# Four orders of work dealt anew in a block-recurrent attention and SwiGLU kernel: middle batches, last batch and states

## The chip, the cores and the metric

The kernel runs on one core of one Trainium2 chip. The time is the device time of one execution in microseconds (us). TensorE (PE, with its weight loads PEld), VectorE (DVE), ScalarE (ACT), GpSimd (POOL) and SyncE (SP, which here only issues DMAs) run side by side, each through its own instructions in order, and wait for one another through semaphores.

## The reference, cut to what matters

```python
# x (8, 8, 512, 64) and state (8, 8, 32, 64); scale = 1 / 8
a  = softmax(scale * x @ state^T)     # over the 32 state rows
xread = a @ state                     # 512 rows a batch and head
a2 = softmax(scale * state @ x^T)     # over the 512 tokens
sread = a2 @ x                        # 32 rows a batch and head
y  = concat([xread, sread], axis=2)   # 544 rows a batch -> (4352, 512)
n  = y / sqrt(mean(y * y) + 1e-6) * rms_g
g, v = n @ w_gate, n @ w_val          # (512, 1536) each
out = (g * sigmoid(g) * v) @ w_out    # (1536, 512)
```

All of it is float32.

## The kernel before, in words

The work goes batch by batch (b = 0 to 7; the 512 token rows of each), and the 256 state rows of all batches come at the end. Batch 0 is computed while the weights are converted, with an order of its own (`ORDER`). From batch 1 on, a batch has two stages, and the attention of the next batch is woven into them.

Hidden stage (`hidden_seven`, L704). The 12 column blocks of the hidden layer are taken in six pairs, mp = 0 to 5. Gate and value products of a pair are built by a scheme with seven half-size products instead of eight, so each pair needs seven products of 128x256 on TensorE (L714, stream h), sums of its weight blocks (vs, L594 to L597 on GpSimd), sums of the token blocks (`slot_sums`, L632 to L635 on GpSimd), three adds on the way out (L776 on VectorE), three copies out of PSUM (L760, L763, L765 on ScalarE, stream t), a Silu (L767) and two multiplications into hb (L789). Pairs 3 to 5 also form sums for the next stage (L795, L801). The banks in PSUM are few: two for x, one for y, one for z, so a product waits until the copy or add of an earlier one has read its bank. Token weights of a batch are its own: `own_weights` (L555) multiplies state rows into the weights (L567, TensorE), ScalarE copies the result to v (L579).

Projection stage (`project_twice`, L985). hb times w_out by the same scheme applied twice: seven outer products o, each of seven inner ones of 3 x 2 matmuls of 128x128 (L1016, stream p). Each outer product needs four quarter sums (L1064, L1066, L1068, L1070 on VectorE, stream k, in two buffers), some need half sums (L1075). Results p1, u2, p5 and c21 are copied to `kept` tiles (L1026, ScalarE), added to (L1056, VectorE), combined by four adds on GpSimd (L1042, L1044, L1046, L1047) and stored (L1124, SP queue). The `kept` tiles of p1, u2 and c21 share two buffers with g of the hidden stage, so a copy into g waits for a store.

Attention of batch b+1 (`tokens_read` L403, stream a; `states_read` L457, stream s): x goes through VectorE transposes (L328) and a round trip through DRAM (L330, L335: four transfers into xG on the ScalarE queue) to the scores (L345), softmax steps on VectorE (L354 to L433), the read (L440), squares (L447), their sum (L450 to L389), the root on GpSimd (L289), its spread over rows (L296) and the scaling (L453); the states' read is L509, with a transpose at L524.

Queues: SP issues, in its own order, the weights w_m of a pair (`fetch`, L187, 1 MB each, three buffers), the quarter sums of w_out (`fetch_quarters`, L962, three buffers), the stores, the state rows (L127) and x (L132).

The order of all this is written out by hand: each step of each stream is one letter in a string, and the loop takes the next step of the stream that the letter names. A letter thus fixes an instruction's place on its own engine against the other streams; it holds no engine back for another. `FIRST` is the order of batch 1, `PERIOD` of batches 2 to 6, `LAST` of batch 7, `STATES` of the state rows. `LAST` has no next batch: its stream a is the norm of the states (L532 to L547, L699) and the first sums of w for the states (L671 to L677). In `STATES`, y is the other sums of w and p, c, k are those of `project_seven` (L862: products L879, adds L924 and L931, copies L916).

| letter | stream | engine |
|---|---|---|
| h, t, u | products, copies with Silu, sums of the hidden stage | PE, ACT, DVE |
| v, x | own weights: products; copies and sums | PE; ACT and POOL |
| w | slot sums and first own weights of the next batch | POOL, PE |
| p, c, k, o | projection: products, copies, sums, stores | PE, ACT, DVE, SP |
| a, s | attention of the next batch | all |
| f, g, l | fetches of weights, of quarter sums; loads of x and states | SP |
| y | sums of w for the states | DVE |

Of the kernel before, what the change touches and what calls it, by code (L numbers as in the profile page):

```python
# [28 lines left out]
)  # L29

PERIOD = (
    "vfhththahhtalhhuxxutthufxtvhhhtahahuuuuuthauhattahhhhxthhuxuutxhuhuttuvkkxxxvxha"
    "hhthhauuuxxhkaatuhkuuthuaattaaahuahuhuthtsusushhhuutthhughuuptpaauufhuagpkuppkkp"
    "saakfgkkappcpkpakkckpkppapppppckkkkpakppppppkppkpppcaaaaaksssaaaaakpppckkpppksap"
    "pkskkagggcksakaakppppaooaoposkppppgkkkpasakoawsswxosspxfxlccoowxxxf"
)

FIRST = (
# [4 lines left out]
    "xosspxfxlccoowxxxf"  # L43
)
LAST = (
    "vfhththhhthhuxxutthufxtvhhhthhuuuuuthuhtthhhhxthhuxuutxhuhuttuvkkxxxvxhhhthhuuux"
    "xhktuhkuuthuattahuhuhuthtuuhhhuutthhughuuptpuufhuagpkuppkkpkfgkkppcpkpakkckpkppp"
    "ppppckkkkpkppppppkppkpppcakaakpppckkpppkppkkkgggckkakppppooopokppppgkkkpakoopcco"
    "o"
)  # L50
STATES = (
    "hyyyyhthyytthhhuuhtuhththhytuuhuuhthuhhtthyuhyyutyhhhuuuttyuhhutyyhhthuhyhuhuttu"
    "yhuhttyuhuhuuhuthhyuthythytuhuuhuhutuuphuupcpkpcpukkcpkpkpc"
)


# [1191 lines left out]
```

## Time and profile before

| what | us |
|---|---|
| median of three runs | 770.23 |
| the three runs | 770.18, 770.23, 770.73 |
| the profiled execution, its own time | 770.64 |
| its span, first to last instruction | 768.9 |
| PE busy in the span | 752.1 |
| DVE busy | 608.3 |
| ACT busy | 350.5 |
| POOL busy | 292.0 |
| first L714 product of batches 3, 4, 5, 6 | 305.8, 387.5, 469.2, 551.4 |
| granted TensorE clock, share of full speed | 1.000 |

Busy time is the time in which an engine has an instruction at work; a matmul that is held inside TensorE's pipeline counts as busy. The timeline gives, for each group of equal instructions, start and length in us, and in brackets the idle time before it with the instruction whose end released it. A group of matmuls ends later than the next one starts, since they are pipelined: the distance from start to start is the time that TensorE spends on a group. One matmul of the program in float32 shows as two records.

### The profile page before, as it was taken

Reading aid. Unit: us, or ns where it says so; the run is one execution under the profiler, and the core shown is the slowest. Engines: PE = TensorE matmul, PEld = TensorE weight load, DVE = VectorE, ACT = ScalarE, POOL = GpSimd, SP = SyncE. Lnnn points to the kernel's source line nnn. Section 1 sums busy time; section 2 is a strip of 40 time slices with the busy share of each in tenths; the row PEclk is TensorE's granted clock in tenths of the full one; section 3 lists DMA queues with packets and bytes.
Section 4 is the critical chain, followed back from the end, with each engine's and each line's share of the span. In section 5 each row is a group of like instructions: output and inputs, shape, how many; then the busy total and the mean of one; then the engine's idle time right before and its main releaser. Section 6 shows DMA issues by size and latency. Waiting matters only on the chain.

```text
span 768.9 us, 14347 instructions
## 1 busy us (share of the span) xinstructions
PE 752.1 (98%) x5608; PEld 595.0 (77%) x5608; DVE 608.3 (79%) x1000; ACT 350.5 (46%) x548; POOL 292.0 (38%) x379
## 2 busy tenths in 40 slices
PE   8899999999999999999999999999999999999998
PEld 7534434778877898879977997889878988899996
DVE  4999997589956996689957994799569975799562
ACT  5898974544245513653165424542355136511220
POOL 2000002984584226632474039402842266325400
PEclk9999999999999999999999999999999999999999
DMA  9787845745786167825683467616862665052311
GB/s 291 213 284 258 312 180 194 276 154 209 268 252 238 41 233 244 292 55 202 202 304 116 127 216 253 228 52 231 250 238 51 233 206 217 1 202 73 124 55 27
DMA packets 61890, 146.15 MB, mean 190 GB/s; under 512 B 15744, under 2 KB 32640, under 8 KB 54912
## 3 DMA queue, kind: packets, MB, share of 16 engines
q1 hardware_dynamic: 48704, 125.78, 47.8%
q10 hardware_dynamic: 13120, 19.47, 8.8%
q8 instruction: 44, 0.72, 0.4%
q14 instruction: 22, 0.18, 0.1%
HBM read 116.46 MB, written 28.77 MB: 189 GB/s over the span
## 4 chain that ended last, share of the span: by engine, by line
PE 62%; DVE 27%; POOL 4%; issue 3%; ACT 2%; DMA 1%; SPq 0%; DVEq 0%; ACTq 0%; POOLq 0%
PE f L714 26%; PE f L1016 14%; PE f L816 6%; PE pv L610 5%; DVE hb L789 3%; DVE hb L1075 3%; PE at L567 3%; PE f L879 2%; DVE h L1070 2%; PE pv L567 2%; DVE g L776 2%; DVE h L1064 2%; DVE hs L795 2%; DVE h L1066 2%; DVE kept L1056 1%
## 5 line engine op out<-in xcount | busy, mean ns | idle before, releaser
L714 PE MATMUL f<-aT_s,v 128*128 128x256 f32 x504 | 117.5, 380 | 0.0
L714 PEld LDWEIGHTS f<-aT_s,v 128*128 128x128 f32 x504 | 95.2, 190 | 18.5 <-ACT v L579 5.0
L776 DVE TENSOR_TENSOR g<-g,f 128x512 f32<-128x512 f32 (+1 forms) x96 | 61.9, 650 | 53.4 <-PE f L714 42.1
L1042 POOL TENSOR_TENSOR kept<-kept 128x256 f32<-128x256 f32 x28 | 23.5, 839 | 199.7 <-DVE z L428 113.1
L714 PE MATMUL f<-aT_t,vs 128*128 128x256 f32 x336 | 87.7, 385 | 0.9 <-ACT g L760 0.5
L767 ACT ACTIVATE hb<-g 128x1024 f32<-128x1024 f32 (+1 forms) x48 | 48.3, 1006 | 70.8 <-DVE g L776 70.7
L1016 PE MATMUL f<-w,h 128*128 128x128 f32 x588 | 75.3, 278 | 3.6 <-DVE h L1066 3.5
L714 PEld LDWEIGHTS f<-aT_t,vs 128*128 128x128 f32 x336 | 61.9, 190 | 19.3 <-issue 7.8
L1016 PEld LDWEIGHTS f<-w,h 128*128 128x128 f32 x588 | 69.8, 192 | 5.7 <-DVE h L1066 4.8
L1026 ACT COPY kept<-f 128x512 f32<-128x512 f32 (+1 forms) x56 | 28.9, 540 | 71.5 <-PE f L1016 56.2
L594 POOL TENSOR_TENSOR vs<-v 128x256 f32<-128x256 f32 x42 | 32.6, 776 | 68.0 <-ACT v L579 68.0
L579 ACT COPY v<-pv 128x512 f32<-128x512 f32 x42 | 22.7, 592 | 76.2 <-PE pv L567 76.2
L289 POOL TENSOR_TENSOR ri<-ss,mhalf 128x4 f32<-128x4 f32 x8 | 10.4, 1295 | 116.3 <-DVE ss L371 113.8
L714 PE MATMUL f<-aT_t,v 128*128 128x256 f32 x168 | 44.5, 387 | 1.5 <-DVE c L776 1.5
L816 PE MATMUL f<-wo,hb 128*128 128x512 f32 x96 | 44.4, 600 | 0.0
L765 ACT COPY g<-f 128x512 f32<-128x512 f32 (+1 forms) x48 | 26.9, 560 | 37.8 <-PE f L714 37.8
L610 PE MATMUL pv<-aT_s,v 128*128 128x512 f32 x96 | 43.7, 597 | 0.3 <-ACT t L616 0.3
L714 PE MATMUL f<-aT_s,vs 128*128 128x256 f32 x168 | 43.8, 383 | 0.0
L789 DVE TENSOR_TENSOR hb<-hb,f 128x512 f32<-128x512 f32 (+1 forms) x48 | 31.2, 650 | 15.9 <-PE f L714 15.4
L789 DVE TENSOR_TENSOR hb<-hb,c 128x512 f32<-128x512 f32 (+1 forms) x48 | 40.6, 845 | 3.5 <-ACT hb L767 3.3
L1016 PE MATMUL f<-wo,h 128*128 128x128 f32 x336 | 42.1, 275 | 0.0
L1016 PE MATMUL f<-wo,hb 128*128 128x128 f32 x336 | 42.1, 275 | 0.0
(179 smaller groups left out, 1689.2 us busy)
## 6 DMA issues: line engine op xcount, KB each, us to landing
w_m<-w_d SPq DMA_DIRECT2D x48, 1024.0 KB, 6.6
w<-t_d SPq DMA_DIRECT2D x49, 576.0 KB, 4.1
out_dram<-kept SPq DMA_DIRECT2D x56, 128.0 KB, 3.3
raw<-in_moe_w_val_dram SPq DMA_DIRECT2D x6, 1024.0 KB, 6.0
raw<-in_moe_w_out_dram SPq DMA_DIRECT2D x6, 1024.0 KB, 7.1
w_d<-w_m SPq DMA_DIRECT2D x6, 1024.0 KB, 4.9
x_b<-in_x_dram SPq DMA_DIRECT2D x6, 1024.0 KB, 7.6
x_d<-xB ACTq DMA_DIRECT2D x6, 1024.0 KB, 4.6
```

Source lines behind the costliest of these rows:

```text
L567: TE.matmul(out=pv[e][Ns * j:Ns * j + Ns, :], lhsT=stT_g[b][D * e:D * e + D, j, :], rhs=w[D * e:D * e + D, j].rearrange("p m k f -> p (m k ...
L594: GE.tensor_tensor(out=vs[:, 0], in0=a21, in1=a22, op=ALU.add)
L610: TE.matmul(out=to[0], lhsT=lhs(i, k), rhs=r, start=(i == 0), stop=(i == len(rhs) - 1))
L714: TE.matmul(out=ps[:, i, 0:half], lhsT=l[:, i, :], rhs=r, start=(start and i == 0 and k == 0), stop=(k == len(lhs) - 1), skip_group_check= ...
L765: SE.copy(gates(q)[1], q["x"][:, :, 0:half])
L767: SE.activation(out=hb[:, 2 * mp:2 * mp + 2, 0:n].rearrange("p m (c t) -> p m c t", c=2), in_=q["g"][:, :, :, 0:half], func=ACTF.Silu if s ...
L776: VE.tensor_tensor(out=to, in0=to, in1=q[ps][:, :, 0:half], op=ALU.add)
L789: VE.tensor_tensor(out=part, in0=part, in1=val, op=ALU.mult)
L816: TE.matmul(out=banks[r], lhsT=hb[:, m, P * r:P * r + P], rhs=wo[:, m, :], start=(m == 0), stop=(m == NM - 1))
L1016: TE.matmul(out=to[half][:, slot, :], lhsT=lhs[:, k, :], rhs=rhs[:, k, :], start=(fresh and n in (0, 4) and k == 0), stop=(k == QM - 1), s ...
L1026: SE.copy(k[:, 4 * i:4 * i + 4 - i], banks[name][i])
L1042: GE.tensor_tensor(out=k[:, 1:3], in0=k[:, 0:1].to_broadcast([P, 2, QD]), in1=k[:, 1:3], op=ALU.add)
```

## The change

Three strings are replaced; no function is touched. `FIRST` and `ORDER` stay. The letters of each string are the same in number, so each stream has the same steps; only their places differ. By the change's own description, the plan behind the new strings lets VectorE and GpSimd take turns at SBUF.

```diff
 PERIOD = (
-    "vfhththahhtalhhuxxutthufxtvhhhtahahuuuuuthauhattahhhhxthhuxuutxhuhuttuvkkxxxvxha"
-    "hhthhauuuxxhkaatuhkuuthuaattaaahuahuhuthtsusushhhuutthhughuuptpaauufhuagpkuppkkp"
-    "saakfgkkappcpkpakkckpkppapppppckkkkpakppppppkppkpppcaaaaaksssaaaaakpppckkpppksap"
-    "pkskkagggcksakaakppppaooaoposkppppgkkkpasakoawsswxosspxfxlccoowxxxf"
+    "vlhhatthhtaxxhvuxuthhthuhtauuhhtuhuhuthtahtuaaahuhhtuhuhuxhxtutxhthukkkhtaakavfx"
+    "xxvgahuhuthuuuxhthhuuxtahtaaaaahuaxhuthhtuhhthhthhsppusuuuuffutaauuhpsspuppppukp"
+    "ukkkkckkaakkgppkkcpppakooskakakakkppppacpppappppcckpfppcakakapppaakkkasskkgkaagg"
+    "pppppppppppaakakkooakgapssskaaakkkoosspppcfpaawwsslpssxxxpcoowxxxfg"
 )
...
 LAST = (
-    "vfhththhhthhuxxutthufxtvhhhthhuuuuuthuhtthhhhxthhuxuutxhuhuttuvkkxxxvxhhhthhuuux"
-    "xhktuhkuuthuattahuhuhuthtuuhhhuutthhughuuptpuufhuagpkuppkkpkfgkkppcpkpakkckpkppp"
-    "ppppckkkkpkppppppkppkpppcakaakpppckkpppkppkkkgggckkakppppooopokppppgkkkpakoopcco"
+    "vhthtfhtxhghuuthhhttvuuhhtxxuhhuuthhthtauhhtuuhhxxxuutvvhhtuuhthxxxhtxxxuhhuuthu"
+    "fhthtuuhuuhthukhuhugtuhthhthhkkhuuuthuuutukahauugpupppppckkkkkkkkkkpppppappakcpk"
+    "kkkkkkkkkkakppapppgpgppppppppoccppkpccppppppkpppkppkppaapkkkppggokpkpffookkoccoo"
     "o"
 )
 STATES = (
-    "hyyyyhthyytthhhuuhtuhththhytuuhuuhthuhhtthyuhyyutyhhhuuuttyuhhutyyhhthuhyhuhuttu"
-    "yhuhttyuhuhuuhuthhyuthythytuhuuhuhutuuphuupcpkpcpukkcpkpkpc"
+    "hththtyyhuhuhhttuhhhyyytyuhutuhhhutthtuyyhhuuyhhthhhuyututyyyhhtyuhhthuuuhhuhtth"
+    "ythuuuyyyutuhuhuytuuyhthhuuhthtuhuhutuuppkhpuucppkkccpkpkpc"
 )
```

What moves on each engine, from the built program (no instruction is added or taken away; GpSimd's order is the same):

- TensorE, batches 2 to 6: L307 one product earlier; the L567 group of mp 3 three products earlier, the groups of mp 4 and 5 one product later; L345 one product earlier; the first two steps of the projection stay ahead of the last hidden product; L440 one L1016 step later; at the end of the batch L567 of the next batch's first pair goes ahead of L509, and one L1016 step stands between L509 and L524.
- VectorE: the four quarter sums of the first outer product together, after pair 2; the sums of pairs 4 and 5 later; L416, L426, L431 and L433 woven between the quarter sums; L491 after L440's place; the squares' sums (L450) after the quarter sums of outer product 5.
- ScalarE: copies of v for mp 2 before the first Silu; the xG transfers around the copies of mp 4.
- SP: the four state rows and a quarter fetch ahead of the first weight fetch; p1's stores right after its combination.
- Last batch: L547 and L699 before p1's adds; the quarter sums of outer products 3 and 4 in one row; the sums of w for the states later; u2's adds at the very end of the batch's sums. L537 stands just ahead of the last hidden product.
- States: no sums of w before the first copy; the second projection product and the first L931 around the last hidden product.

## The prediction

> **What bounds the kernel now.** I read the page's busy shares first, then the table by stage (one batch, the last batch, the states), then TensorE's waits in each stage, then the timelines of the places those waits name.
>
> ```profile
> PE 752.1 (98%) x5608; PEld 595.0 (77%) x5608; DVE 608.3 (79%) x1000; ACT 350.5 (46%) x548; POOL 292.0 (38%) x379
> ```
> ```profile
> 387.54:469.22 81.68, 81.29 (x664) 68.21 (x663) 66.36 (x115) 34.89 (x59) 34.73 (x46) 1.00 0.60 198
> 633.11:711.00 77.89, 76.56 (x544) 68.93 (x544) 60.82 (x93) 27.75 (x44) 34.80 (x44) 1.00 0.35 124
> 711.00:768.90 57.90, 54.22 (x404) 51.53 (x404) 27.51 (x56) 11.66 (x28) 8.62 (x9) 1.00 0.21 69
> ```
>
> TensorE (the first busy figure after stretch and length) sets the end at full clock: in a middle batch it shows 81.29 of 81.68 us. No matmul is added or removed, so the change can win only TensorE's waits, and lose by making new ones. The waits are larger than the idle column says, since a matmul that waits inside the pipeline counts as busy. The timeline of batch 3's projection (start, length, then what) shows it:
>
> ```profile
> 363.01 0.83 PE L1016 MATMUL f<-w,hs 128*128 128x128 f32 x6
> 364.24 1.60 PE L1016 MATMUL f<-w,h 128*128 128x128 f32 x12 [0.39 <-DVE h L1066]
> 365.68 1.50 PE L1016 MATMUL f<-wt,h 128*128 128x128 f32 x12
> ```
>
> Six records take 0.67 from start to start (1.34 for twelve elsewhere). Here 363.01 to 364.24 is 1.23, and the next twelve take 1.44: 0.66 lost, though only 0.39 is called a wait. Counted this way, start to start, batch 4 loses 0.18 at its second products (389.09), 0.34 around 423.5 to 425, 0.66 at the fourth product's quarter sum and 0.20 shortly after: **1.38 us a batch**. What is late at 364.24 is the VectorE chain, which had run without a gap since 345:
>
> ```profile
> 353.71 1.82 DVE L1075 TENSOR_TENSOR hb<-hs,hb 128x768 f32<-128x768 f32 x2
> ...
> 359.50 2.35 DVE L1075 TENSOR_TENSOR hb<-hb 128x768 f32<-128x768 f32 x2
> 361.77 0.81 DVE L1064 TENSOR_TENSOR h<-hs 128x384 f32<-128x384 f32 x1
> 362.50 1.21 DVE L431 TENSOR_TENSOR eS<-eS,z 128x512 f32<-128x512 f32 x1
> 363.64 0.55 DVE L1066 TENSOR_TENSOR h<-h,hs 128x384 f32<-128x384 f32 x1
> ```
>
> The pair on L1075 took 1.82 alone and 2.35 while GpSimd ran L1042 to L1047 (358.88 to 363.17); with L1064 (0.81 against 0.55) and L431 (1.21 against 0.69) GpSimd cost this chain 0.53 + 0.26 + 0.52 = 1.3 us. The other large wait stands where the last batch meets the states:
>
> ```profile
> 707.29 1.17 POOL L1047 TENSOR_TENSOR kept<-kept 128x256 f32<-128x256 f32 x1
> ```
> ```profile
> 710.77 0.37 ACT L760 COPY g<-f 128x256 f32<-128x256 f32 x1 [2.37 <-POOL kept L1044]
> 711.03 0.38 ACT L763 COPY c<-f 128x256 f32<-128x256 f32 x1
> 711.19 0.97 PEld L714 LDWEIGHTS f<-x_t,v 128*128 128x128 f32 x8 [1.72 <-ACT g L760]
> ```
>
> The copy into g needs the buffer of the kept tile of u2. GpSimd ends u2's combination at 708.46, its two stores follow, and the copy starts 2.3 later: I read the releaser as the store, not the L1044 named. TensorE loses 1.6.
>
> **What the Trainium skill says.** "GPSIMD Engine Reference", section 1 Specifications: GpSimd's SBUF interfaces are shared with VectorE, with contention against VectorE instructions that have two SBUF inputs. The trace agrees in the 1.3 us above, and in L789, 845 ns with both inputs in SBUF against 650 with one in PSUM. The same page, section 4.1: GpSimd is about twice as slow on two-input operations; here 128x256 takes 0.73 on GpSimd and 0.42 on VectorE. "DMA: Bandwidth & Descriptors", Anatomy of one DMA — SWDGE (gpsimd) path: some 2.0 us fixed per transfer, for a path that these stores don't take. The stores here, on SP's hardware queue, land 2.0 to 2.1 after issue at best and 3.3 in the median; I use those for when a store frees a buffer.
>
> **The change part by part.** T is time from a batch's first L714 product (387.47 in batch 4). I put TensorE's new order end to end at the pitches above (0.864 for an L714 step, 0.67 for an L1016 step, 1.22 for an inserted L567 group, 2.07 for two, 1.49 for L345, 1.24 for L440), and at each place where TensorE needs another engine added up that engine's instructions since its own last wait.
>
> *TensorE's floor.* 81.68 - 1.38 = 80.30. One more change of shape is added (L1016 between L509 and L524); L389 and L524 cost the L1016 step behind them 0.08 to 0.09, L567 about 0.2 in and out: take 0.2. **80.5.**
>
> *Start of a batch.* L307 comes one product earlier, so the second product on x starts at T 2.1 instead of 1.8; ScalarE's copy of the first (0.97 + 0.25 + 0.57) is done at 1.8 and GpSimd's second sum about 1.0: the 0.18 goes. Slot sums and vs stand as before, since u2's combination ends at about T -3.5 in both. The group for mp 3 moves from T 7.4 to 4.7; its weights land at T 2.5 to 3.9 (391.22 and 309.36 among the landings): hidden, 0.8 spare. On SP the four state rows (3.4 us of issue) and one quarter fetch now stand ahead of mp 5's weights: issued near T 10, landed 7 to 8 later, needed at 23. The next quarter fetch waits on L1016 until T 45 and holds two weight fetches behind it, needed after T 75: nothing. The p1 stores go out 8 to 10 us earlier.
>
> *Scores.* L345 stands one product earlier, near T 29.6 instead of 30.55. The fourth xG transfer lands 6.8 to 7.2 after the first is issued; ScalarE issues the first at T 23.15 instead of 23.74. It lands between 30.0 and 30.3, and L345's second half wants it at 29.85; v's last copy is there at 29.6. Bounds 0 and 0.5; take **0.2 added**. The 0.34 of before (waits for g and c copies of mp 5) goes: these copies have no step in front of them now.
>
> *Projection.* After c+=x of mp 5 (41.7) VectorE has 0.6 + 0.1 + 0.6, then hb at 43.4 to 44.0 behind the last product, needed at 44.4. Then quarter sums of product 1, the half sums, those of product 2, L416 and the first L1056, up to 51.2. The second L1056 waits for TensorE's 51.1 and ends at 51.85. From there to product 3's second quarter sum: 0.87 + 0.6 + 0.87 + 0.37 + 0.46 + 0.6 + 0.46 = 4.23, with GpSimd's turns 5.3 to 5.6: done at 57.2 to 57.5, TensorE wants it at 57.8. The 0.66 goes. What is late next: the fourth quarter sum (59.3 to 59.6 against 59.8), L440 (62.1 against 62.5), L389 (71.4 to 71.8 against 71.8), L296 (74.5 against 74.8), L524 (tie). All are met by 0 to 0.4 only, so I charge 0.5 for those that slip. The 0.20 behind the old wait goes.
>
> Sum for a batch: 80.5 + 0.2 + 0.5 = 81.2 against 81.68, so **-0.5, five times: -2.4**. Batch 5's extra 0.5 (82.20; a store that landed late) I leave standing.
>
> *Last batch.* It shows one wait of 0.19. L547 and L699 (3.15 on VectorE) move ahead of p1's adds; product 3's second quarter sum then ends at 57.1, wanted at 57.9. **0**; if that cover goes, up to 0.6.
>
> *Junction.* L1056 for u2 now stands behind the quarter sums of product 6 with nothing after it, and is bound only by product 5's end, 4.7 before the last product's. It ends 4.1 before; GpSimd needs 2.2 more alone and 2.9 beside VectorE's sums of w; stores land 2.1 to 2.5 later, at +0.3 to +1.3 after the batch's end, and the copy is wanted at 1.2: 0 to 0.3 stays of 1.6. **-1.3.**
>
> *States.* The half difference of L931 runs under the last L714 product: the 0.22 at 753.48 goes. **-0.2.** The end (copy, store, 3.4 us) is as before.
>
> Sum: -2.4 - 1.3 - 0.2 = -3.9 on the profiled execution's 770.64 (span 768.9), which lies 0.4 above the median of 770.23. The same difference from the median: **766.4**.
>
> **Rivals.** (a) *Slower: VectorE falls behind in the projection.* The margins there are 0.2 to 0.4, and the turns were priced from one stretch at 1.3. If the new alignment makes them cost twice that, 1.3 more, each batch waits 0.9 to 1.2 at product 3 or at L389 instead of 0, and as VectorE has hardly a gap from T 41 to 75 nothing wins it back: 81.2 - 0.5 + 2.0 = 82.7, five times +1.0, less 1.5: 773.7. It decides once VectorE loses more than 1.0 beyond my sum. For it: VectorE is busy 66.4 of 81.7 and the margins are thin. Against: the instructions that meet GpSimd are nearly the same ones as before. (b) *The same: waits move.* xG's landing takes 0.5, late stores of c21 at mp 1 0.4, L389 and L524 0.4: 81.8 a batch, five times +0.1, less 1.5: 769.2. (c) *All margins hold*: 80.6 a batch, -5.4 - 1.5 - 0.5: 762.8. That the order isn't followed is no rival: the built program shows the instructions in the new order.
>
> **How the numbers follow.** About 0.2% (1.5 us) is what a measurement can tell from no change. Forecast 0.57, (c) 0.11, (b) 0.19, (a) 0.13. Faster is forecast and (c): 0.68; same 0.19; slower 0.13. The range 764.0 to 771.0 leaves out most of (a) and (c), just under 0.2, and takes in (b) and both ends of xG's and the margins' costs (five times 0 to 0.5 each).
>
> **What would show it.** Right: batches of 81.0 to 81.4 between their first products; no 0.39 wait for L1066; a wait below 0.4 for the states' first copy. Wrong: a batch over 81.7 with TensorE waiting for L1066, L1070, L386 or xG.

## The result, and the profile after

The first comparison gave 765.25 us (median of seven executions, 762.37 to 767.18) against 770.73 before: a ratio of 0.9926, 95% interval 0.9908 to 0.9943. Five of the seven executions ran with a granted clock of 0.995 or 0.996 in the records and are some 3 us longer for it; this falls on the kernel before too (22 of 104 executions), and ahead of batch 1 (last section). The changed kernel run again had 762.81 (761.94 to 763.43) against 771.45, ratio 0.9881 (0.9861 to 0.9901). So the change is worth some 8.5 us, the forecast said 3.9, and the first median came near the forecast because the clock took 3 us of the gain.

Busy times on the page after:

```profile
PE 746.6 (98%) x5608; PEld 595.5 (78%) x5608; DVE 598.0 (79%) x1000; ACT 351.6 (46%) x548; POOL 292.5 (38%) x379
```

The table by stage (stretch, length, then busy time of PE, PEld, DVE, ACT, POOL, granted clock, DMA share, GB/s) for a middle batch, the last batch and the states:

```profile
384.29:464.46 80.17, 80.17 (x671) 68.22 (x663) 64.54 (x115) 35.17 (x59) 34.80 (x46) 1.00 0.59 202
624.78:699.70 74.92, 74.92 (x537) 67.31 (x529) 55.25 (x89) 27.00 (x42) 34.03 (x41) 1.00 0.38 136
699.70:756.08 56.38, 56.08 (x422) 53.37 (x420) 30.76 (x59) 12.06 (x28) 9.91 (x10) 1.00 0.21 70
```

In the middle batches TensorE's busy time is the whole stretch, the trace names no wait of TensorE in them any more, and batch after batch has the same length. VectorE's busy time fell by 1.8 a batch (66.36 to 64.54) with the same 115 instructions. The place that the prediction showed first, product 3's quarter sums in TensorE's timeline, now runs at an even pace of 1.34:

```profile
439.45 1.50 PE L1016 MATMUL f<-wt,hs 128*128 128x128 f32 x12
440.79 0.83 PE L1016 MATMUL f<-w,hs 128*128 128x128 f32 x6
441.46 1.50 PE L1016 MATMUL f<-w,h 128*128 128x128 f32 x12
442.80 0.39 PE L1016 MATMUL f<-wt,h 128*128 128x128 f32 x2
```

VectorE's timeline there, with GpSimd's L1042 to L1047 at work from 435.51 to 439.52:

```profile
436.01 1.05 DVE L1075 TENSOR_TENSOR hb<-hb 128x768 f32<-128x768 f32 x1
436.98 0.67 DVE L426 TENSOR_REDUCE z<-eS 128x16 f32<-128x512 f32 x1
437.58 0.94 DVE L1075 TENSOR_TENSOR hb<-hb 128x768 f32<-128x768 f32 x1
...
439.07 0.87 DVE L1064 TENSOR_TENSOR h<-hs 128x384 f32<-128x384 f32 x1
439.86 0.68 DVE L431 TENSOR_TENSOR eS<-eS,z 128x512 f32<-128x512 f32 x1
440.46 0.55 DVE L1066 TENSOR_TENSOR h<-h,hs 128x384 f32<-128x384 f32 x1
```

L426 (one input) stands between the halves of L1075, and L431 comes when GpSimd is done: 0.68 where it was 1.21. L1066 ends at 441.01, 0.45 before TensorE wants it. At the junction the states' first copy waits 0.46 for its own product and for no store:

```profile
700.84 0.37 ACT L760 COPY g<-f 128x256 f32<-128x256 f32 x1 [0.46 <-PE f L714]
```

From first product to first product, in us:

| stage | before | after | after, again |
|---|---|---|---|
| batch 1 | 87.63 | 87.62 | 87.75 |
| batches 2 to 6 | 82.20, 81.68, 81.68, 82.20, 81.69 | 80.22, 80.16, 80.17, 80.16, 80.16 | 80.16, 80.16, 80.16, 80.24, 80.16 |
| last batch | 74.67 | 74.92 | 74.92 |
| states, to the end of the last L879 | 57.69 | 56.39 | 56.38 |
| behind it | 3.44 | 4.5 | 3.44 |

The place of each gain inside batch 4 comes from the starts of TensorE's groups, T from the batch's first product. Where the new order has a step more or less ahead of the mark, its pitch (0.864 for an L714 step, 0.67 for an L1016 step) is taken out:

| mark | before | after | shift, steps taken out | lost between marks that goes |
|---|---|---|---|---|
| second L567 group | 21.57 | 22.32, one L714 step more | -0.11 | 0.11 at the second products |
| L714 behind L345 | 31.84 | 30.59, one L714 step fewer | -0.39 | 0.28 at L345 |
| first L1016 | 40.92 | 40.20 | -0.72 | 0.33 at T 36 to 37.4 |
| L440 | 62.67 | 61.96, one L1016 step more | -1.38 | 0.66 at product 3 |
| L389 | 72.05 | 71.14, one L1016 step more | -1.58 | 0.20 behind it |
| batch's end | 81.68 | 80.17 | -1.51 | -0.07, the added change of shape |

The five batches give 8.6 (1.0 of it the 0.5 that batches 2 and 5 had on top in this one execution of before), the junction and the states 1.3; the last batch takes 0.25, and the end of this execution 1.06, which is not there when the changed kernel runs again.

### The profile page after: what moved, and what is told of

Same layout as the page of the kernel before. It is cut to its first block, busy times and chain, and to the rows that moved or that the text cites. A ratio compares the mean times of both kernels' runs of the same rounds, so it can differ in the third digit from the quotient of the medians.

```text
span 760.6 us, 14352 instructions
## 1 busy us (share of the span) xinstructions
PE 746.6 (98%) x5608; PEld 595.5 (78%) x5608; DVE 598.0 (79%) x1000; ACT 351.6 (46%) x548; POOL 292.5 (38%) x379
## 4 chain that ended last, share of the span: by engine, by line
PE 88%; DVE 9%; ACT 1%; issue 1%; POOL 0%; DVEq 0%; POOLq 0%
PE f L714 37%; PE f L1016 27%; PE f L816 6%; PE pv L610 5%; PE at L567 4%; PE pv L567 3%; PE f L879 2%; PE at L509 1%; PE at L345 1%; PE f L1148 1%; PE at L440 1%; DVE h L1070 1%; DVE hb L789 1%; PE at L296 1%; DVE hb L1075 0%
## 5 line engine op out<-in xcount | busy, mean ns | idle before, releaser
L714 PE MATMUL f<-aT_s,v 128*128 128x256 f32 x504 | 119.1, 382 | 0.0
L714 PEld LDWEIGHTS f<-aT_s,v 128*128 128x128 f32 x504 | 94.7, 190 | 23.2 <-issue 10.1
L776 DVE TENSOR_TENSOR g<-g,f 128x512 f32<-128x512 f32 (+1 forms) x96 | 62.3, 653 | 50.7 <-PE f L714 45.3
L1042 POOL TENSOR_TENSOR kept<-kept 128x256 f32<-128x256 f32 x28 | 24.0, 856 | 174.6 <-DVE kept L1056 172.5
L714 PE MATMUL f<-aT_t,vs 128*128 128x256 f32 x336 | 87.1, 383 | 0.5 <-DVE g L776 0.5
L1026 ACT COPY kept<-f 128x512 f32<-128x512 f32 (+1 forms) x56 | 29.6, 532 | 125.4 <-PE f L1016 83.1
L1016 PE MATMUL f<-w,h 128*128 128x128 f32 x588 | 74.9, 277 | 1.6 <-DVE h L1066 1.5
L714 PEld LDWEIGHTS f<-aT_t,vs 128*128 128x128 f32 x336 | 62.6, 190 | 15.5 <-POOL vs L594 4.2
L1016 PEld LDWEIGHTS f<-w,h 128*128 128x128 f32 x588 | 69.7, 192 | 6.4 <-issue 4.1
L594 POOL TENSOR_TENSOR vs<-v 128x256 f32<-128x256 f32 x42 | 31.3, 746 | 81.2 <-ACT v L579 81.2
L714 PE MATMUL f<-aT_t,v 128*128 128x256 f32 x168 | 43.8, 383 | 1.3 <-DVE c L776 1.3
L714 PE MATMUL f<-aT_s,vs 128*128 128x256 f32 x168 | 43.7, 383 | 0.0
L776 DVE TENSOR_TENSOR c<-c,f 128x512 f32<-128x512 f32 (+1 forms) x48 | 31.3, 652 | 15.2 <-PE f L714 15.2
L789 DVE TENSOR_TENSOR hb<-hb,f 128x512 f32<-128x512 f32 (+1 forms) x48 | 31.0, 646 | 14.6 <-PE f L714 14.6
L1016 PE MATMUL f<-wo,h 128*128 128x128 f32 x336 | 42.1, 275 | 0.0
L1016 PE MATMUL f<-wo,hb 128*128 128x128 f32 x336 | 42.1, 275 | 0.0
L1016 PEld LDWEIGHTS f<-wo,hb 128*128 128x128 f32 x336 | 40.3, 192 | 0.4
```

What stands on the lines that cost most here:

```text
L594: GE.tensor_tensor(out=vs[:, 0], in0=a21, in1=a22, op=ALU.add)
L714: TE.matmul(out=ps[:, i, 0:half], lhsT=l[:, i, :], rhs=r, start=(start and i == 0 and k == 0), stop=(k == len(lhs) - 1), skip_group_check= ...
L776: VE.tensor_tensor(out=to, in0=to, in1=q[ps][:, :, 0:half], op=ALU.add)
L789: VE.tensor_tensor(out=part, in0=part, in1=val, op=ALU.mult)
L1016: TE.matmul(out=to[half][:, slot, :], lhsT=lhs[:, k, :], rhs=rhs[:, k, :], start=(fresh and n in (0, 4) and k == 0), stop=(k == QM - 1), s ...
L1026: SE.copy(k[:, 4 * i:4 * i + 4 - i], banks[name][i])
```

## The experiments

Each was timed in five rounds beside the kernel before. The table has batch 4's length and the shift of each mark against before, steps taken out as above, so that a row reads from left to right as what TensorE has won by there.

| run | batch 4 | second L567 | behind L345 | first L1016 | L440 | L389 | end |
|---|---|---|---|---|---|---|---|
| whole new order | 80.17 | -0.11 | -0.39 | -0.72 | -1.38 | -1.58 | -1.51 |
| new head | 80.40 | -0.11 | -0.38 | -0.73 | -1.28 | -1.27 | -1.28 |
| VectorE's new head alone | 81.00 | 0 | -0.27 | -0.28 | -0.69 | -0.68 | -0.68 |
| two quarter sums moved | 81.07 | 0 | -0.27 | -0.61 | -0.61 | -0.61 | -0.61 |
| new tail | 81.25 | 0 | 0.04 | 0.01 | -0.29 | -0.49 | -0.43 |
| L431 moved by one place | 81.69 | 0 | 0.05 | 0 | -0.60 | 0.01 | 0.01 |
| GpSimd's p1 sums left out | 80.83 | 0 | -0.22 | 0.01 | -0.65 | -0.85 | -0.85 |

**Middle batches alone, ends alone.** `PERIOD` new with the old `LAST` and `STATES`, and the reverse.

```diff
-PERIOD = (before)          period_only
+PERIOD = (after)
-LAST, STATES = (before)    ends_only
+LAST, STATES = (after)
```

> Orders of batches 2 to 6 new, last batch and states as before. Theory T: the gain is TensorE's waits in batches 2 to 6, all gone, 80.2 us from first product to first product where before has 81.7 (82.2 in batches 2 and 5), whatever the ends do: span 8.3 to 8.6 less than before at full clock, near 760.3; and the part lost again in the medians is the granted clock, which falls to 0.995 to 0.997 once TensorE has no pauses left: then near 763, time 764 to 766, with a spread of some us. Rival R1: the clock has to do with the ends or with the chip of that day, then clock 1.00 here and a time of 762 with a spread under 1 us. Rival R2: the batches lean on the new ends, then less than 7 us of the span.

> Orders of the last batch and of the states new, batches 2 to 6 as before. Theory T: the states' first copy no longer waits (1.3 less), the last batch is 0.2 longer, the tail behind the last L879 about 1 longer for its last store stands on another footing: sum between -1.3 and 0, 769.4 to 770.7; clock 1.00 and spread under 1 us, because the middle batches keep their pauses. Rival R1 (clock from the ends): clock 0.996 here and a time over 771. Rival R3: the longer tail came from the profiled run alone, then -1.3 in full.

Middle batches alone: 763.82 against 771.78, ratio 0.9895 (0.9875 to 0.9916), all five at 80.16 to 80.19, span 760.3. The ends alone: 770.49, ratio 0.9987 (0.9975 to 0.9999); states 56.39 for 57.69, last batch 74.92 for 74.67, the tail behind the last L879 3.4 as in before (rival R3). So the batches don't lean on the ends; R2 falls. Of the clock the first expectation was wrong: one execution in six of the dense kernel had 0.996, and of before, with all its pauses, 9 in 33.

**Head and tail of the batch.** The new order up to `u`'s last step with the old one behind it, and the reverse; steps that stand on different sides go with the tail or the head of the string named first.

```diff
-PERIOD = before[: last u] + before[rest]
+PERIOD = after[: last u] + before[rest]     head_new
+PERIOD = before[: last u] + after[rest]     tail_new
```

> In batches 2 to 6 the steps up to the last step on hidden's products stand as before, and all steps behind it (projection, its copies, combinations, stores, the next batch's normalisation) in the new order. Theory T (two seats of loss, each with its own cause): the 0.66 at product 3's second quarter sum and the 0.20 behind it go, 0.9 to 1.0 a batch (80.7 to 80.8), the 0.34 and 0.18 of the hidden stage stay: about -4.7, 766, clock 0.997 to 1.00. Rival H (VectorE enters the projection late, so that the hidden stage's order is what counts): at most 0.4 a batch, time over 768.5.

> The counterpart: steps up to the last step on hidden's products in the new order, all behind as before. Theory T: 0.34 and 0.18 go, the wait for product 3's second quarter sum stays between 0.3 and 0.7: 0.5 to 0.8 a batch (80.9 to 81.2), about -3, 767.5. Rival H: 1.2 or more a batch, time under 764.5. If both halves together give clearly less than the new order whole, they lean on each other.

My theory fell here, and the figures are near those of rival H. New head: 764.85, ratio 0.9908 (0.9891 to 0.9926), 80.41 a batch. New tail: 769.21, ratio 0.9968 (0.9953 to 0.9984), 81.25. With the projection's own order untouched, the wait at product 3 shrank from 0.66 to 0.1 (from first L1016 to L440 the row goes from -0.73 to -1.28), so the place where TensorE waits is not the place where all of the time is lost. What the places share is VectorE. In the kernel before, its timeline around T 22 to 30 of batch 4:

```profile
410.46 0.56 DVE L1066 TENSOR_TENSOR h<-h,hb 128x384 f32<-128x384 f32 x1
413.02 1.48 DVE L776 TENSOR_TENSOR g<-g,f 128x512 f32<-128x512 f32 x2 [2.00 <-PE f L714]
414.68 0.69 DVE L776 TENSOR_TENSOR c<-c,f 128x512 f32<-128x512 f32 x1 [0.18 <-PE f L714]
415.28 0.96 DVE L1068 TENSOR_TENSOR h<-hb 128x384 f32<-128x384 f32 x1
416.16 1.21 DVE L789 TENSOR_TENSOR hb<-hb,c 128x512 f32<-128x512 f32 x1
417.30 1.07 DVE L1070 TENSOR_TENSOR h<-hb,h 128x384 f32<-128x384 f32 x1
```

There is a hole of 2.0 us ahead of 413.02, and from 414.68 on not one until product 3 at 445. The third and fourth quarter sum of product 0 stand behind the hole, where GpSimd is at its sums of v (L594 to L597): 0.96 and 1.07 instead of 0.55.

**The two quarter sums.** Two letters of before, moved into the hole:

```diff
-    ...hhuxuutxhuhuttuvkkxxxvxha" "hhthhauuuxxhkaatuhkuuthuaatt...
+    ...hhuxuutxhuhuttuvkkkkxxxvx" "hahhthhauuuxxhaatuhuuthuaatt...
```

> The kernel before with two letters moved: the third and fourth quarter sum of product 0 (L1068, L1070) stand right behind the second, in a hole of 2.0 us that VectorE has at T 23.5 to 25.5, and no longer in its chain from T 25.5, where they took 0.96 and 1.07 beside GpSimd's sums of L594 and VectorE then had no gap up to product 3. Theory Q: that chain is what is late at product 3 and at mp 5's products, so that nearly 1 us a batch goes with these two letters alone: 0.56 to 0.66 at product 3 and some or all of the 0.33 at T 36 to 37.4; 80.6 to 81.0 a batch, about -4.5, time near 766 to 767. Rival S: ScalarE's and TensorE's order in the hidden stage (copies of v, the transfers of xG, L345 one product earlier) brought the gain of the new head, and VectorE follows: 0 to 0.3 a batch, time over 770.

769.32 against 771.03, ratio 0.9971 (0.996 to 0.9983); three of five batches at 81.07, two at 81.4 to 81.5 where xG landed later. VectorE's timeline has them at 0.55 each, and a gap behind:

```profile
410.58 0.55 DVE L1068 TENSOR_TENSOR h<-hb 128x384 f32<-128x384 f32 x1
411.05 0.55 DVE L1070 TENSOR_TENSOR h<-hb,h 128x384 f32<-128x384 f32 x1
412.66 1.48 DVE L776 TENSOR_TENSOR g<-g,f 128x512 f32<-128x512 f32 x2 [1.06 <-PE f L714]
```

All that went, went by the first L1016: the loss at T 36 to 37.4 was VectorE's, not ScalarE's copies', against what rival S and the prediction hold. The 0.27 at L345 needs an early xG as well (it landed at T 30.45 here, 30.78 in before), but an early xG alone wins nothing: in batch 2 of before L345 took 1.02 too, and from the second L567 group to the first L1016 it was 19.36, as in batch 4 (19.35). But TensorE's wait at product 3 stayed, 0.40 in its timeline:

```profile
444.95 1.27 PE L1016 MATMUL f<-w,h 128*128 128x128 f32 x9 [0.40 <-DVE h L1066]
```

I read its length as VectorE's work between hidden's last products and product 3: these start earlier for both engines now, so it doesn't change. Theory Q was half right: the place, not the size.

**One letter at the wait itself.** L431 behind L1066 in the kernel before.

```diff
-    "...kckpkppapppppckkkkpakppppppkppkpppcaaaaaksss..."
+    "...kckpkppapppppckkkkpkappppppkppkpppcaaaaaksss..."
```

> The kernel before with one letter moved by one place: L431 (1.21 us in the profile) stands behind product 3's second quarter sum L1066 and no longer ahead of it. Both theories: the 0.66 there goes whole, as VectorE is then 1.2 early; what is behind may take some back (L440, L389). By the table of waits -0.66 to -0.86 a batch, 80.8 to 81.0, time near 767; if VectorE's lateness only moves on to L440 or to the fifth product, under 0.3 a batch, time over 770.

770.99, ratio 1.0 (0.9988 to 1.0012): both theories wrong. The wait for L1066 goes and L440 is reached 0.60 earlier, but its second half waits for the second transpose into aT_s. VectorE's line in its timeline, then TensorE's:

```profile
449.56 0.71 DVE L433 STREAM_TRANSPOSE aT_s<-eS 128x512 f32<-128x512 f32 x1
```
```profile
449.85 1.13 PE L440 MATMUL at<-aT_s,rows 32*64 32x512 f32 x5
450.35 0.66 PE L440 MATMUL pv<-aT_s,rows 32*64 32x512 f32 x4
450.81 0.60 PE L440 MATMUL at<-aT_s,rows 32*64 32x512 f32 x3
```

The 0.60 is given back at once: here, inside a stretch without a gap, moving one step only moved the wait. That is no rule: the new tail deals such a stretch anew (VectorE has no gap from T 27 on there either, and L440 stands one L1016 step later) and wins 0.43.

**GpSimd's turns.** p1's four sums on GpSimd are left out, once in the kernel before and once in the changed one; the output then lacks these sums.

```diff
+            if what != "p1":
                 GE.tensor_tensor(...)   # L1042 to L1047, four of them
```

> The kernel before, with GpSimd's four sums of p1's combination left out (the output misses them; copies and stores stay). Theory (the prediction's price): GpSimd's turns cost VectorE's chain 1.3 just ahead of product 3's second quarter sum (L1075 2.35, L1064 0.81, L431 1.21), so that without them L1066 comes 1.3 earlier: the 0.66 goes and perhaps the 0.20 behind it, 80.8 to 81.0 a batch, -3.4 to -4.4. If these durations come from something else (shape, banks), they stay at 2.35, 0.81 and 1.21 and the time at 771.

> The changed kernel, with GpSimd's four sums of p1's combination left out (the output misses them). In the kernel before, leaving them out won 0.85 in each of batches 2 to 6 and 1.4 in batch 1. Theory: the new order pays GpSimd's turns out of VectorE's slack, so batches 2 to 6 stay at 80.16; batch 1, whose order is the old one, loses its 1.4, and the last batch the 0.24 that it waits at product 3: span 758.3 to 758.6 against 760.0, time near 761. Rival: VectorE still sets the end of the batches somewhere, and they shorten by 0.2 or more each: span under 757.5.

In the kernel before: 764.91, ratio 0.9907 (0.9883 to 0.9931), 80.83 a batch. VectorE's timeline in place of the lines in the prediction (the numbers of lines are one higher):

```profile
438.27 1.81 DVE L1076 TENSOR_TENSOR hb<-hb 128x768 f32<-128x768 f32 x2
440.00 0.55 DVE L1065 TENSOR_TENSOR h<-hs 128x384 f32<-128x384 f32 x1
440.47 0.68 DVE L431 TENSOR_TENSOR eS<-eS,z 128x512 f32<-128x512 f32 x1
441.07 0.55 DVE L1067 TENSOR_TENSOR h<-h,hs 128x384 f32<-128x384 f32 x1
```

1.81, 0.55 and 0.68 where it was 2.35, 0.81 and 1.21: the turns cost 0.54 + 0.26 + 0.53 = 1.33, as priced, and the 0.66 and the 0.20 go. This is what the Trainium skill's "GPSIMD Engine Reference", section 1 Specifications, says of instructions with two SBUF inputs. Batch 1 is 1.4 shorter as well and the states 0.6, so that the time fell by more than the 3.4 to 4.4 expected. In the changed kernel the batches stay at 80.16 without GpSimd's sums, so there the turns are paid out of slack; the last batch falls from 74.92 to 74.67, so there they are not. The median, 763.42 (ratio 0.9888, 0.9861 to 0.9916), is no better than the changed kernel's, since three of its six executions had the lower clock. Batch 1, from which I expected 1.4 as in the run on before (86.22), gave 0.1 to 0.3 (87.49): it reaches L389 1.1 earlier than the changed kernel run again and loses 0.9 from the start of the last L567 group on (2.77 to the batch's end, where the run on before has 1.88). Why is open.

**VectorE's order alone, and xG's transfers.** The head's new order for VectorE with every other engine's as before; then the same with ScalarE's four transfers of xG in a row ahead of v's copies.

```diff
-ScalarE: v4 v4 v5 xG0 g1 xG1 v5 xG2 xG3       head_dve, as before
+ScalarE: xG0 xG1 xG2 xG3 v4 v4 v5 g1 v5       dve_xg
 VectorE, both: L1068 L1070 in the hole; L414, L416 of the scores ahead of mp 5's sums
```

> The kernel before with VectorE's order alone taken from the new head: all other engines' letters up to hidden's last product keep their order. Against the run that moved only the two quarter sums (81.07 a batch) it also moves L416 of head 0 and L414 of head 1 (0.6 each) out of VectorE's chain behind mp 5's products, which ends at product 3. Theory V (what is late at product 3 is the sum of VectorE's work from hidden's last product to there): the 0.56 there goes as well, 80.4 to 80.6 a batch, about -5.5, time 765 to 766; what stays is L345's wait for the fourth transfer of xG (0.2 to 0.5) and 0.1 at the second products. Rival S (the order of ScalarE's exponentials and copies behind it counts): product 3's wait stays, 81.0 a batch, 768 to 769.

> As the run with VectorE's order of the new head alone, and ScalarE issues the four transfers of xG (L335) in a row ahead of v's copies, 1.5 to 2.5 us earlier; L345 stays where it was. Theory X: in before the fourth transfer lands 7.0 after the first is issued, 0.2 after L345's first product, and L345 loses 0.2 to 0.5 by it; landing earlier, L345 takes 1.02 and the batch 0.2 to 0.5 less than in the run beside it (80.1 to 80.3). Rival Y: L345's longer stretch is its own pace at that place, or v's copies, now 1.7 later, make TensorE wait at the L714 behind: the same or more than beside it.

VectorE alone: 768.62, ratio 0.9961 (0.9946 to 0.9977). Product 3's wait shrinks by 0.41 (first L1016 to L440: -0.28 to -0.69), where theory V had 0.56, but the 0.33 at T 36 to 37.4 is back. I put that down to L416, which now stands ahead of L776 while L345, which starts it all, comes as late as before. So it is 81.0, not 80.5: the total that rival S gave, though not in the places that it named. With xG early as well: 767.27, ratio 0.9943 (0.9923 to 0.9963), all five batches at 81.00, where the run beside it had 81.19 and 81.57 in two. In batch 4 the fourth transfer of xG landed 3.0 earlier (T 27.5 against 30.5), and L345 took the same 1.02. In the two longer batches of the run beside it the transfer landed at T 30.7 and 31.0, and L345 took 1.23 and 1.61: its landing explains these, and theory X's 0.2 to 0.5 holds for them alone. In the kernel before, L345's late landing in batch 3 (the L714 behind it at T 32.10 against 31.84 in batch 4) was made up by the first L1016, at 40.92 in both: VectorE was the later one anyway. The 0.6 from here to the new head (81.00 to 80.40) is by subtraction the part of the other engines: L345 one product earlier, so that VectorE's transposes (L354) come earlier too, L307 (0.11), and the other steps of TensorE, ScalarE and SP. These are not taken apart.

One rival to the hole stays open. VectorE's own work shrinks wherever TensorE wins: its busy time in batch 4 is 66.4 in before, 65.9 with the two sums moved, 65.4 with its new head, 65.6 with the new tail, 65.1 with the whole new head and 64.5 with the whole order, as its sums meet fewer of GpSimd's. Of the 2.03 that the two sums took in the chain, 0.93 was GpSimd's share, and 1.10 is what fills the hole. No run separates the two, the hole and the collisions spared. Less work alone is not enough: with L431 moved VectorE is busy for 66.0, and the batch is as long as before.

**The last batch.** L547 and L699 back behind product 3's quarter sums.

```diff
-LAST: "...tukahauugpupppppckkkkkkkkkkpppppappakcpk" "kkkkkkkkkkakppapppgpg..."
+LAST: "...tukahauugpupppppckkkkkkkkkkpppppappkcpkk" "kkkkkakkkkakppapppgpg..."
```

> The changed kernel, with L547 and L699 of the last batch put back behind product 3's quarter sums (one letter). The last batch has 74.92 where before has 74.67, 0.24 of it at product 3's second quarter sum, where VectorE is late by L547, L699 (3.15) and by GpSimd's turns. Theory: 74.7 again, the junction still without a wait, 0.2 less than the changed kernel; span 760.3, or 759.3 if the last store's landing (1.87 against 0.85) was of that one execution. It can't be told in the median, only in the profile's stages. Clock: if the granted clock of 0.996 falls on some executions of every kernel, also on some of before, it comes here as often as there; if a TensorE without pauses brings it, on most of these runs and on none of before.

The last batch is 74.67 again, but the states take 57.08 instead of 56.38. VectorE comes to u2's adds later, and the wait at the junction, which was expected to stay away, is partly back:

```profile
701.85 0.37 ACT L760 COPY g<-f 128x256 f32<-128x256 f32 x1 [1.85 <-DMA out_dram<-kept]
```

0.25 won, 0.7 lost: no version to keep. The median (763.19, ratio 0.989, 0.9864 to 0.9917) can't tell it from the changed kernel, and the span of 761.2 has a tail of 4.75 in it. The releaser is now named as the store, as the prediction had read it.

**The changed kernel again.**

> The changed kernel once more, unedited, on this chip. Open are the clock and the tail. If the granted clock of 0.996 falls on any kernel's executions by chance (one in five of before, of the runs with pauses, and of those without), it comes here in one of five and the median is 762 to 763.5, 8 less than before; if a TensorE without pauses brings it, in most of the runs, and the median is 765. The tail behind the last L879 is 3.4 as in before and in the run with only the ends new, if the 4.5 was the landing of one store in one execution; 4.5 again if it belongs to the new order.

762.81, ratio 0.9881 (0.9861 to 0.9901), none of five executions at the lower clock. The tail is 3.44. In the first profile the last four stores (L1131) landed 2.6 to 2.8 after issue, here 1.5 to 1.7, as in before; with the last batch put back it was 2.9 to 3.1. So the longer tail belongs to single executions. (The 1.87 and 0.85 named for the last batch's run are the lengths of the records of issue, not the landings.)

## Why the prediction was half right

The sign and the places were right: 0.18, 0.34, 0.66 and 0.20 were named as what goes, and 0.11, 0.33, 0.66 and 0.20 went; the junction's wait went. The size was wrong: -0.5 a batch was forecast and -1.5 came, and the chain of VectorE behind several of the waits was followed back only to 345. By its steps:

- **TensorE's floor, 80.5.** It came out at 80.16, by two terms. The waits of before were 1.58, not 1.38: L345's own stretch was taken as pitch (1.49 for L345), while 0.28 of it was a wait. A group's pitch has to come from where nothing can wait for data. And the added change of shape cost 0.07 instead of 0.2.
- **xG, 0.2 added.** The step took ScalarE's first issue to be at T 23.15; it came at 22.49, the fourth landed at 29.05, and L345 wanted it at 29.6. Nothing was added.
- **Margins, 0.5 charged.** None slipped. L1066 of product 3 was forecast to end at T 57.2 to 57.5 and ended at 56.7. From the second L1056 to there I had 5.3 to 5.6 with GpSimd's turns; it was 4.9, because L426 and L431 come at times when GpSimd takes less from them. Price and mechanism of the turns were right (1.33 by leaving them out); what of them falls on the new order was overstated by 0.4 to 0.7. Charging 0.5 for margins beside it counted the same doubt twice.
- **T 36 to 37.4.** Forecast to go because ScalarE's copies have no step in front of them. It goes, but with VectorE's two sums alone, ScalarE's order untouched. "Had run without a gap since 345" was true and too short a look back: from 414.68 in batch 4, T 27, there was none. Followed to its start, the gapless stretch leads to the hole ahead of it, and it runs through three of the losses (T 36 to 37.4, product 3, the 0.20 behind it).
- **Batch 5's extra 0.5, left standing.** It arises ahead of the second L567 group (T 22.08 instead of 21.57) and belongs to single executions: the run that moved L431, with this part of the order as in before, had 81.67 to 81.69 in all five batches. The prediction's reading, a store that landed late, was right: of the two `kept` stores issued at T 5.2 and 5.6 the later landed at T 8.9 in batch 5 and 7.6 in batch 4, the copy L760 into g waited 2.08 for it instead of 0.68, and TensorE lost 0.5 behind that copy. In the five profiles with the new `PERIOD` none of these stores landed later than T 8.05, and no batch lost time there; whether the new order would bear a landing at 8.9 isn't shown.
- **Last batch, 0.** It took 0.25: the second quarter sum ended at T 58.0, not 57.1. That sum left out GpSimd's turns, which the middle batches' had: L1075 took 2.64 instead of 1.82, L1066 0.97 instead of 0.55. The prediction's "up to 0.6 if that cover goes" was the right case.
- **Junction and states, -1.5.** -1.3, from other parts. The junction won 1.79, where 1.3 was forecast, and L931's place 0.08, where 0.2 was. A wait that the prediction did not have takes 0.57 back: 12.1 into the states a product (L714) waits for VectorE's L789, and VectorE had just spent 1.48 and 1.37 on the sums of w (L671, L673) beside GpSimd's L982.
- **Three figures.** The `kept` stores land 1.7 after issue at best, not 2.0 to 2.1. L789's 845 against 650 are means over two shapes: of the 42 of 128x512 in before with both inputs in SBUF half took no more than 693 ns and the longest 1484, and those with one in PSUM 643 to 690. And 3.9 less than 770.23 is 766.3, not 766.4.

At the full clock the time is what rival (c), all margins hold, gave: 762.8. That is in part luck too: its batches have 80.6, not 80.16, and before is 771.45 beside the second measurement, not 770.23. Rival (a), turns at twice the price, has nothing for it. That the first median lies at 765.25, beside the forecast, is the clock's doing.

## What to carry to other kernels

When a saturated engine waits for a second one at several places, follow the second one's gapless stretch back to its last hole and see what work fits there: the place where the wait shows up may only be where the debt falls due. Here two sums moved into the hole won up to 0.61 a batch, and one step moved at the wait itself won nothing. If two engines share access to SBUF, price the instruction pairs that really overlap in the new order, in every stage: last batch and states each lost time to pairs that were left out. And charge doubt once.

## What the runs showed of the hardware

- **A dip of the clock in the prologue.** Of the executions of before that were timed beside the experiments, 22 of 104 had a mean clock of 0.995 or 0.996 and took 3 us more (on one chip a median of 774.4 against 771.4); of the changed kernel it was five of seven on one chip and none of five on another. Of the 14 profiles two have it, that of the new tail and that of the changed kernel without GpSimd's p1 sums. Rows by stretch as above, the first of the latter (mean clock 0.995):

```profile
20.00:40.00 20.00, 18.00 (x97) 11.71 (x96) 19.81 (x30) 15.32 (x20) 1.02 (x1) 0.86 0.69 198
```
The second of the changed kernel run again (mean clock 1.0):

```profile
20.00:40.00 20.00, 17.82 (x99) 10.39 (x97) 19.85 (x28) 16.22 (x21) 1.02 (x1) 1.00 0.72 212
```

Between 20 and 40 us the clock is 0.86 against 1.00, and batch 1 starts at 139.5 instead of 136.6; batch 4 has 80.16 in both. In narrower stretches it is a clock of 0.50 for 6.83 us, from 34.53 to 41.36 here and from 34.70 to 41.53 with the new tail. Half of 6.83 is 3.4, an estimate of what it can cost. The strings that were changed come into play from batch 2 on, so the new order doesn't bring it. In these two profiles the record of a full clock starts latest, 7.2 and 7.4 us into the span, and in the other twelve at 4.3 to 6.7. So it may hang on when an execution starts; that wasn't tried.
- **Both sides pay for SBUF.** GpSimd's L1044 took 1.32 beside VectorE's L1075 and 0.73 with VectorE elsewhere; VectorE's quarter sum L1068 took 0.96 beside GpSimd's L595 and L596, and 0.55 alone; L596 took 1.04 there instead of 0.73.
